# Attention in four steps per pair of heads with a fixed TensorE order, scores and masks on 64x64 quarters of the array

## The chip, the cores and the metric

One NeuronCore of a Trainium2 chip runs the whole program: TensorE (PE; its weight loads are listed as PEld), VectorE (DVE), ScalarE (ACT), GpSimd (POOL) and the queue that issues DMAs (SP). The metric is the device time of one execution in microseconds. The kernel before takes 1002.98 us (median of 3 runs, 1002.25 to 1003.76).

## The reference

Four stages follow each other: causal attention with a linear memory, gated together; a bilinear layer; its two output products; and a last layer with `h - tanh(h)`.

```python
# q, k, v: (4, 8, 576, 64); B*H = 32 heads, taken in 16 pairs
scores = scale * q @ k.T;  scores = where(causal, -1e9, scores)
a = exp(scores - max);  a /= a.sum(-1) + 1e-9;  local = a @ v
q_p = where(q > 0, q, exp(q) - 1) + 1
mem_out = (q_p @ M_prev) / (q_p . z_prev + 1e-6)
x = g * mem_out + (1 - g) * local          # rows: 2304 tokens x 512
h = ((x @ w1) * (x @ w2)) @ w3;  x = h @ w_out     # d_ff 1024
h = x @ w_in;  out = (h - tanh(h)) @ w_out2        # d_ff 2048
```

`w3 @ w_out` does not depend on the tokens; the kernel computes that product once ("the fold") while attention runs. The weights arrive as 64-bit floats and are decoded on the chip into a high and a low part (three products replace one).

## The kernel before

**Attention.** A pair P holds two heads on the two halves of the partitions. Its 576 query rows are five tiles u = 0 to 4 (four of 128 rows, one of 64), tile u sees 128 x (u+1) keys (tile 4 all 576). One unit (P, u) does: `scores` (one matmul per head, in fp32, which shows as two passes in the trace; then the causal mask is added by a matmul of a bf16 identity with a mask tile), `rmax` (DVE, L346), `exps` (ACT, L355, with its sum), `norm` (two small DVE operations L364 and L365, then POOL multiplies, L372), `trans` (transposes of the 128x128 blocks of p by PE, L404, L411 and L415; copies from PSUM into tiles g by ACT or DVE, L383 and L385) and, after tiles 1 and 4, `av` (p times v, tile o, copied out into xs). Scores have two PSUM buffers of two banks each (tile sc), the transposes two banks (t), and o shares two banks with the fold (fo).

**Shape of a matmul on the array.** The trace gives rows*columns of the array: 64*128 for the scores of tiles 0 to 3 (two heads side by side on the two row halves), 64*64 for those of tile 4, 128*128 for masks, transposes and fold, 128*64 for `av`, and 64*64 for its last block.

**The fold and other background.** A generator `early` is advanced 1.85 steps per unit: it decodes w_out and w3 (items of four steps: POOL L72 and L75, ACT L77 and L79, DVE L82, POOL L94 with DVE L97), issues the fold's matmuls (12 per item, tile fo), then decodes the first four of the 16 tiles of w1 and w2 and does the memory part of the first group of 384 tokens (tiles mw, mq, mt, mo; result added into xs on DVE, L532).

**After attention** the 2304 tokens go in six groups of 384: `stage` splits xs into xh and xl, `ab_pe` forms the products with w1 and w2 (tile ab), `ab_chain` multiplies them, `x2_pe` multiplies by the fold (tile x). Group 0 also waits for the other twelve decoded tiles of w1 and w2 (wa, wb), whose place in SBUF is attention's. Then come the last layer's two products (h and o).

**What sets the order.** The program is traced in the order of the loop over units (letters S E N T L G A with lags), and a scheduler reorders the instructions of each engine while it keeps the dependencies. So TensorE's order is the scheduler's: it fits transposes, fold pieces and the first products of group 0 between the units.

Of the kernel before, what the change touches and what calls it, by code (L numbers as in the profile page):

```python
# [33 lines left out]
def block_kernel(ctx, tc, qk, qt, vt, mp, zp_d, beta, w1, w2, w3t, wo, wi, wo2, ident_d, mask_d, out):  # L34
# [109 lines left out]

    def mm(o, lhsT, rhs, start, stop):
        return PE.matmul(o, lhsT, rhs, start=start, stop=stop).ins  # L146

    PU = 1
    PB, RB = 5, 3
    HIA, HF = 1, 1  # L150
    ZX = ("z5", "z6", "z7", "z8", "z9", "zA", "zB")
    NZ = len(ZX)
    PL = "PPPPPPPPPPG"
    HG = 4
    SB = 2
    ST = 1
    NV = "PPPPP"
    FG = 1
    G1 = 1
    DW = 1  # L160
    HIP = 1
    ORDER = "SENTLGA"
    LAG = {'S': 0, 'E': 0, 'N': 0, 'T': 1, 'L': 0, 'G': 0, 'A': 2}
    WI = ()
    PO_, PA = "xzw", "r1234"
    OP, FL = 5, "V"
    SN, XP, MR = 2, (), 0
    TH = (("V", 0), ("A", 0))
    NE, EM, BG = 4, 1, 1.85
    BG2, MB = 1.85, 40  # L170
    MS, FS, FS5 = 4, 3, 6
    CPA = (0, 1, 3, 4)

    att = ExitStack()
    PW = [256, 512, 768, 1024, 576] if PU else [1024] * 5
    apl = {}
    for x in PA:
        apl[x] = att.enter_context(tc.tile_pool(name="ap" + x, bufs={"1": 1, "2": 2, "r": RB,
                                                                     "3": 1 if PU else PB, "4": 6}[x]))
    ap1, ap2, apr, ap3, ap4 = [apl[x] for x in "12r34"]  # L180
    identb = ap1.tile([128, 128], BF16, name="identb")
    maskb = ap1.tile([128, 192], BF16, name="maskb")
# [27 lines left out]
    etags = [f"{x}{f}" for f in range(NE // 2) for x in ("wa", "wb")][len(WI):]  # L210
    otags = ztags[:4] + etags[:4]
    FO, fv = {}, {}

    def fold_o_item(j):
        def dst():
            FO[j] = slot(otags[j])
            return FO[j][:, 0], FO[j][:, 1]

        return wo[j], dst

    def fold_item(f, half):
        def dst():
            t = wslot(ap1, "zs")
            fv[f, half] = t
            return t[:, 0], t[:, 1]

        return w3t[8 * half + f], dst

    def fold_work(psum):
        seq = [("o", j) for j in range(4)]  # L230
        for f in range(8):
            if f >= OP:
                seq += [("o", 4 + f - OP)] if 4 + f - OP < 8 else []
            seq.append((f, 0))
        seq += [("o", j) for j in range(12 - OP, 8)]
        for f in range(8):
            seq += [("x", i) for i, x in enumerate(XP) if x == f]
            seq.append((f, 1))
        make = {"o": fold_o_item, "x": lambda i: w_items[i]}
        dec = Decoder([make[k[0]](k[1]) if k[0] in make else fold_item(*k) for k in seq], DW, 3)  # L240
        yield
        part = {}
        for half in range(2):
            for f in range(8):
                while dec.done <= seq.index((f, half)) or half and dec.done <= seq.index(("o", 7)):
                    dec.step()
                    yield
                acc = psum()
                t = fv.pop((f, half))
                for j in range(4):  # L250
# [5 lines left out]
                    if j % FG == FG - 1:  # L256
                        yield 1
                if half == 0:
                    part[f] = wslot(wfp, f"wf{f}", F32)
                    AC.activation(out=part[f][:, 0], in_=acc, func=AF.Copy)  # L260
                else:
                    s = ap1.tile([128, 512], F32, tag=f"s{f % SN}", name="s")
                    DV.tensor_tensor(out=s, in0=acc, in1=part[f][:, 0], op=ALU.add)
                    WF[f] = wslot(wfp, f"wf{f}")
                    AC.activation(out=WF[f][:, 0], in_=s, func=AF.Copy)
                    (DV if FL == "V" else PO).tensor_tensor(out=WF[f][:, 1], in0=s, in1=WF[f][:, 0].bitcast(F32),
                                                            op=ALU.subtract)
                    yield 2

    if True:  # L270
# [5 lines left out]
        SP.dma_start(out=mraw[:, 0:192], in_=mask_d)  # L276
# [4 lines left out]
        AC.activation(out=maskb, in_=mraw[:, 0:192], func=AF.Copy)  # L281
# [34 lines left out]
        units = [(P, u) for P in range(16) for u in range(5)]  # L316
        sc_t, p_t, st_t, g_t = {}, {}, {}, {}

        mark = {"V": {}, "A": {}}

        def scores(n):
            P, u = units[n]
            q, k = qk_t[P][:, 0], qk_t[P][:, 1]
            hr = [(h, slice(64 * h, 64 * h + 64)) for h in range(2)]
            sc = sc_t[n] = pss.tile([128, 2, 512], F32, tag="sc", name="sc")
            if u < 4:
# [5 lines left out]
            else:  # L332
# [4 lines left out]
                mm(sc[:, 1, 224:288], identb, maskb[:, 128:192], False, True)  # L337

        def seen(n):
            P, u = units[n]  # L340
            return sc_t[n][:, :, 0:128 * (u + 1) if u < 4 else 288]

        def rmax(n):
            P, u = units[n]
# [4 lines left out]
        def exps(n):  # L349
# [7 lines left out]
            sc_t.pop(n)  # L357

        def norm(n):
            P, u = units[n]  # L360
            hp = P % 4
            st, p = st_t.pop(n), p_t[n]
            w = 2 if u < 4 else 1
# [616 lines left out]
```

## Time and profile before

| | us |
|---|---|
| median of 3 runs | 1002.98 |
| profiled execution, its own time | 1002.86 |
| span from first to last instruction | 1001.1 |
| TensorE busy | 967.1 (97%) |
| VectorE, ScalarE, GpSimd busy | 661.3, 634.6, 408.9 |
| mean granted TensorE clock | 0.998 |

The profiled execution is 0.12 us from the median, and 1.8 us of it lie outside the span. Attention's scores end at 247 us, its last product with v starts at 267 us, group 0 ends at 332 us, the six groups at 598 us; the rest is the last layer. TensorE's busy time is counted from the moment an instruction holds the engine, its own weight load and the emptying of the array included, so a busy TensorE can still lose time at each change of shape.

### The profile page before, as it was taken

The numbers are of one execution on the slowest core, as the hardware profiler recorded it, in microseconds if no ns is written. First come the engines' busy times: TensorE is split into PE (matmuls) and PEld (weight loads), VectorE is DVE, ScalarE is ACT, GpSimd is POOL, SyncE is SP. The second block draws the span as 40 slices with busy tenths as digits, with TensorE's granted clock in tenths as the row PEclk, the third lists the DMA queues.
The fourth block names the chain that finished last, engine by engine and source line by source line (L and its number), as shares of the span: only waits on it lengthen the run. The fifth ranks groups of instructions, "written<-read, shape, count | busy, mean of one in ns | idle before, by whom it ended". The sixth has DMA issues, their size and how long they took to land.

```text
span 1001.1 us, 15467 instructions
## 1 busy us (share of the span) xinstructions
PE 967.1 (97%) x5512; PEld 817.0 (82%) x5512; DVE 661.3 (66%) x1185; ACT 634.6 (63%) x1428; POOL 408.9 (41%) x500
## 2 busy tenths in 40 slices
PE   6999999999998999999999999999999999999998
PEld 3565566555786888999999999999899999998996
DVE  4756666786677566442212569788887787888875
ACT  6878766798445544353213668686776777867764
POOL 5856654695367553331001884222222222222222
PEclk9999999999999999999999999999999999999999
DMA  6434533442144553132000100000000000000000
GB/s 232 159 121 138 164 115 124 127 159 64 54 158 151 158 176 106 43 109 81 2 1 1 64 22 1 1 33 1 1 32 1 1 32 1 33 1 1 32 1 32
DMA packets 25804, 68.27 MB, mean 68 GB/s; under 512 B 4864, under 2 KB 5632, under 8 KB 25728
## 3 DMA queue, kind: packets, MB, share of 16 engines
q1 hardware_dynamic: 25728, 67.29, 20.4%
q8 instruction: 43, 0.70, 0.3%
q14 instruction: 33, 0.27, 0.1%
HBM read 62.56 MB, written 4.72 MB: 67 GB/s over the span
## 4 chain that ended last, share of the span: by engine, by line
PE 85%; ACT 5%; DVE 4%; DMA 3%; POOL 1%; issue 1%; SPq 0%; DVEq 0%; ACTq 0%; POOLq 0%
PE o L146 24%; PE h L146 20%; PE ab L146 18%; PE x L146 9%; PE sc L146 5%; PE fo L146 5%; PE t L404 3%; ACT p L355 2%; DMA mw<-in_qt 2%; DVE st L346 1%; DMA r<-in_qk 1%; ACT g L383 1%; PE mo L146 1%; ACT E L79 1%; PE mo L515 1%
## 5 line engine op out<-in xcount | busy, mean ns | idle before, releaser
L860 POOL TENSOR_TENSOR gl<-s,gh 128x384 fp32r<-128x384 f32 x96 | 99.6, 1037 | 288.0 <-ACT gh L854 275.4
L372 POOL TENSOR_SCALAR p<-p,st 128x128 f32<-128x128 f32 (+2 forms) x144 | 92.0, 650 | 59.1 <-DVE st L365 28.6
L146 PE MATMUL ab<-xh,wa 128*128 128x384 f32 x384 | 108.1, 340 | 2.6 <-DVE xs L532 1.4
L146 PE MATMUL x<-abh,wf 128*128 128x384 f32 x384 | 105.8, 340 | 3.4 <-ACT abh L659 3.4
L146 PE MATMUL ab<-xh,wb 128*128 128x384 f32 x384 | 106.9, 337 | 0.1
L836 DVE SCALAR_TENSOR_TENSOR s<-s,u 128x384 f32<-128x384 f32 x96 | 84.2, 877 | 24.9 <-ACT s L826 24.0
L146 PE MATMUL sc<-r 64*64 64x288 f32 (+4 forms) x384 | 77.5, 477 | 15.9 <-ACT p L355 9.4
L355 ACT ACTIVATE p<-sc,st 128x128 f32<-128x128 f32 (+2 forms) x144 | 78.3, 551 | 20.4 <-DVE st L346 18.0
L832 ACT ACTIVATE u<-u,pc 128x384 f32<-128x384 f32 x96 | 59.4, 619 | 46.8 <-DVE s L836 46.7
L656 DVE TENSOR_TENSOR a<-ab,a 128x384 f32<-128x384 f32 x48 | 26.5, 553 | 89.2 <-PE ab L146 85.3
L346 DVE TENSOR_REDUCE st<-sc 128x2 f32<-128x256 f32 (+4 forms) x80 | 64.1, 804 | 21.7 <-PE sc L146 21.2
L146 PEld LDWEIGHTS ab<-xh,wa 128*128 128x128 f32 x384 | 70.0, 188 | 7.4 <-DVE xs L532 2.4
L146 PEld LDWEIGHTS x<-abh,wf 128*128 128x128 f32 x384 | 69.8, 187 | 5.4 <-ACT abh L659 4.3
L824 ACT ACTIVATE u<-h 128x384 f32<-128x384 f32 x96 | 46.7, 487 | 41.5 <-PE h L146 41.5
L842 DVE TENSOR_TENSOR t<-h,t 128x384 f32<-128x384 f32 x96 | 53.2, 554 | 29.8 <-ACT t L825 29.5
L75 POOL TENSOR_SCALAR E<-raw 128x512 f32<-128x512 f32 x72 | 54.8, 761 | 40.0 <-DVE z2p L82 7.6
L146 PEld LDWEIGHTS ab<-xh,wb 128*128 128x128 f32 x384 | 69.9, 188 | 1.1 <-POOL wb L94 0.7
L841 DVE SCALAR_TENSOR_TENSOR s<-s,s 128x384 f32<-128x384 f32 x96 | 63.9, 665 | 8.3
L79 ACT ACTIVATE E<-raw 128x512 uint16<-128x512 uint32 x72 | 56.8, 790 | 17.6 <-POOL E L75 17.3
L72 POOL TENSOR_SCALAR T<-raw 128x512 f32<-128x512 f32 x72 | 51.0, 708 | 39.7 <-DVE zs L97 8.7
L146 PE MATMUL x<-abl,wf 128*128 128x384 f32 x192 | 65.3, 340 | 1.2 <-DVE abl L660 1.2
L146 PE MATMUL ab<-xl,wa 128*128 128x384 f32 x192 | 64.7, 337 | 0.7 <-DVE xl L636 0.7
(214 smaller groups left out, 2569.5 us busy)
## 6 DMA issues: line engine op xcount, KB each, us to landing
raw<-in_wo SPq DMA_DIRECT2D x24, 512.0 KB, 3.7
r<-in_qk SPq DMA_DIRECT2D x15, 576.0 KB, 3.8
raw<-in_w3t SPq DMA_DIRECT2D x16, 512.0 KB, 3.5
raw<-in_w SPq DMA_DIRECT2D x16, 512.0 KB, 3.5
raw<-in_wi SPq DMA_DIRECT2D x16, 512.0 KB, 3.5
v<-in_vt SPq DMA_DIRECT2D x16, 320.0 KB, 3.5
mw<-in_qt SPq DMA_DIRECT2D x18, 256.0 KB, 2.9
out<-ob SPq DMA_DIRECT2D x18, 256.0 KB, 2.3
```

The lines of the kernel that those rows point to most:

```text
L72: PO.tensor_scalar(out=tf, in0=hw, scalar1=TOP, scalar2=-TOP, op0=ALU.min, op1=ALU.max)
L75: PO.tensor_scalar(out=e[:].bitcast(F32), in0=hw, scalar1=2.0 ** -100, scalar2=2.0 ** -53, op0=ALU.mult, op1=ALU.mult)
L79: AC.activation(out=e16, in_=lw, func=AF.Copy, scale=LOW_SCALE, bias=LOW_BIAS)
L146: return PE.matmul(o, lhsT, rhs, start=start, stop=stop).ins
L346: mark["V"][n] = DV.tensor_reduce(out=st[:, 0:2] if u < 4 else st[:, 0:1], in_=seen(n), axis=AX.X if u < 4 else AX.XY, op=ALU.max, negate= ...
L355: mark["A"][n] = AC.activation(out=p[:, x], in_=sc[:, x], func=AF.Exp, bias=st[:, x.start:x.start + 1], accum_out=st[:, 2 + x.start:3 + x. ...
L372: (DV if NV[u] == "V" else PO).tensor_scalar(out=pr, in0=pr, scalar1=sc, scalar2=1.0, op0=ALU.mult, op1=ALU.mult)
L832: AC.activation(out=u, in_=u, func=AF.Relu, bias=pc[:, 2:3])
L836: DV.scalar_tensor_tensor(out=s1, in0=s1, scalar=k2[0], in1=u, op0=ALU.add, op1=ALU.mult)
L841: DV.scalar_tensor_tensor(out=s1, in0=s2, scalar=k2[1], in1=s1, op0=ALU.add, op1=ALU.mult)
L842: DV.tensor_tensor(out=t, in0=o, in1=t, op=ALU.subtract)
L860: PO.tensor_tensor(out=l, in0=s1, in1=h[:].bitcast(F32), op=ALU.subtract)
```

## The change

The loop over 80 units becomes a loop over 64 steps, four per pair: tiles 0 and 1 together (in one score buffer, at columns 0 and 128), then 2, 3 and 4. The matmuls are no longer left to the scheduler: `pinned` marks every matmul and transpose of the attention part, and the marked ones keep the order in which they are written. A step is written as: scores, maximum, exponentials, normalisation; in the third step `av` of the previous pair's tiles 2 to 4, in the fourth `av` of this pair's tiles 0 and 1; one or two fold pieces (three matmuls each); the transposes of the step two before; then background. The fold's decoding (`fold_dec`, 2 steps of it per step, 3 in the first ten) is apart from its matmuls (`fold_pe`, which starts an item two steps after it was decoded), its decoded w3 tile has three buffers instead of one, and the last four w_out tiles have places of their own. The scores of tiles 0 to 3 are four matmuls of 64 rows and 64 columns, and the masks are matmuls on the same quarters (for the second half of the rows only its 64 columns on the diagonal). Tile g1 has two buffers instead of one.

```diff
+    def pinned(i):
+        if in_order[0]:
+            tc.keep_in_program_order(i)
+        return i.ins
+
     def mm(o, lhsT, rhs, start, stop):
-        return PE.matmul(o, lhsT, rhs, start=start, stop=stop).ins
...
+        return pinned(PE.matmul(o, lhsT, rhs, start=start, stop=stop))
+
+    def tp(o, i):
+        return pinned(PE.transpose(o, i, ident))
...
+    ZB, FLAG, WAIT = 3, 2, 2
+    PIECES = (2, 2, 1, 1)
+    PACE, LEAD = 2, 10
...
+    def fold_dec():
+        d = fdec[0] = Decoder([fold_o_item(k[1]) if k[0] == "o" else fold_item(*k) for k in fold_seq], 1, 3)
         yield
+        while d.done < d.total:
+            k = fold_seq[d.done]
+            if k[0] == "o" or len(fv) < ZB or k in fv:
+                n = d.done
+                d.step()
+                if d.done > n and k[0] != "o":
+                    folds.append((k, fstep[0]))
+            yield
+
+    def fold_pe(psum):
         part = {}
         for half in range(2):
             for f in range(8):
-                while dec.done <= seq.index((f, half)) or half and dec.done <= seq.index(("o", 7)):
-                    dec.step()
+                while not folds or folds[0][1] + FLAG > fstep[0]:
                     yield
...
+        GROUPS = ((0, 1), (2,), (3,), (4,))
...
-                K = 128 * (u + 1)
-                for h, r in hr:
-                    mm(sc[:, h, 0:K], q[r, 128 * u:128 * u + 128], k[r, 0:K], True, False)
-                for h, r in hr:
-                    mm(sc[:, h, K - 128:K], identb, maskb[:, 0:128], False, True)
...
+                K = 128 * (u + 1)
+                for h, r, y, c in qs:
+                    mm(sc[c, h, a:a + K], q[r, 128 * u + 64 * y:128 * u + 64 * y + 64], k[r, 0:K], True, False)
+                for h, r, y, c in qs:
+                    mm(sc[c, h, a + 128 * u + 64 * y:a + 128 * u + 128], identb[r, r], maskb[r, 0:128 - 64 * y], False, True)
...
-        for m in range(NU + 8):
-            for x in ORDER:
-                do(x, m - LAG[x])
...
+        for m in range(NM + 4):
+            P, s = divmod(m, 4)
+            fstep[0] = m
+            if m < NM:
+                scores(m)
+                rmax(m)
+                exps(m)
+                norm(m)
+            if s == 2 and P:
+                av(P - 1, 1)
+                if P + 1 < 16:
+                    load_v(P + 1)
+            if s == 3 and P < 16:
+                av(P, 0)
+            for _ in range(PIECES[s]):
+                next(fold, None)
+            if 0 <= m - WAIT < NM:
+                for u in GROUPS[(m - WAIT) % 4]:
+                    trans((m - WAIT) // 4, u)
...
+                    for _ in range(PACE + (m < LEAD)):
+                        next(bg, None)
...
         run(bg)
+        in_order[0] = False
```

TensorE in the last pair, where no fold is left, before (sc scores, maskb and identb the mask matmul, t transposes, o the product with v of the pair's tiles 0 and 1):

```order
L146 MATMUL sc<-r 128x256 x2
L146 LDWEIGHTS identb
L146 MATMUL sc<-maskb,identb 128x128
L146 LDWEIGHTS identb
L146 MATMUL sc<-maskb,identb 128x128
L404 MATMUL t<-ident,p 128x128 x2
L146 MATMUL o<-g_2708,v_104 64x256 x2
L146 MATMUL o<-g_2708,v_104 64x128 x2
L146 MATMUL sc<-r 128x384 x2
L146 LDWEIGHTS identb
L146 MATMUL sc<-maskb,identb 128x128
L146 LDWEIGHTS identb
```

And TensorE after, in the third step of the fourteenth pair (here o is the product with v of the thirteenth pair's tiles 2 to 4):

```order
L153 MATMUL sc<-r 64x512 x4
L153 LDWEIGHTS identb
L153 MATMUL sc<-maskb,identb 64x128
L153 LDWEIGHTS identb
L153 MATMUL sc<-maskb,identb 64x128
L153 LDWEIGHTS identb
L153 MATMUL sc<-maskb,identb 64x64
L153 LDWEIGHTS identb
L153 MATMUL sc<-maskb,identb 64x64
L153 MATMUL o<-g_2611,v_104 64x320 x6
L153 MATMUL o<-g_2611,v_104 64x192 x2
L153 MATMUL o<-g_2612,v_104 64x64 x2
```

The masks moved from two full-array matmuls, a shape of their own between the scores and the product with v, to four on the quarters that the scores use; the product with v stands directly behind the scores.

TensorE at the end of attention before (mt and mo the memory part of group 0, ab the first products of group 0):

```order
L146 MATMUL sc<-r 64x288 x4
L146 LDWEIGHTS identb
L146 MATMUL sc<-maskb,identb 128x64
L515 MATMUL mt<-ident,mw 128x128 x4
L404 MATMUL t<-ident,p 128x128 x2
L146 MATMUL mo<-mq_1497,mc 64x384 x4
L404 MATMUL t<-ident,p 128x128 x8
L146 MATMUL o<-g_2763,v_104 64x320 x6
L146 MATMUL o<-g_2763,v_104 64x192 x2
L146 MATMUL o<-g_2764,v_104 64x64 x2
L146 MATMUL mo<-mq_1498,mc 64x384 x2
L146 MATMUL ab<-xh,wa_2282 128x384
```

The same place after, from the last pair's product of tiles 0 and 1 on:

```order
L153 MATMUL o<-g_3086,v_105 64x256 x2
L153 MATMUL o<-g_3086,v_105 64x128 x2
L156 MATMUL t<-ident,p 128x128 x18
L156 MATMUL t<-ident,p 64x128
L153 MATMUL o<-g_3119,v_105 64x320 x6
L153 MATMUL o<-g_3119,v_105 64x192 x2
L153 MATMUL o<-g_3120,v_105 64x64 x2
L156 MATMUL mt<-ident,mw 128x128 x4
L153 MATMUL mo<-mq_2375,mc 64x384 x4
L153 MATMUL mo<-mq_2376,mc 64x384 x2
L153 MATMUL ab<-xh,wa_2623 128x384
L153 MATMUL ab<-xh,wb_2626 128x384
```

Before, the last pair's transposes and products with v stand among the first ab (the last product with v follows 48 of them); after, all of attention and the third mt come first.

## Rows read from the trace of the kernel before

**Rows 1.** The page: busy time of each engine, and the chain that ended last.

```profile
PE 967.1 (97%) x5512; PEld 817.0 (82%) x5512; DVE 661.3 (66%) x1185; ACT 634.6 (63%) x1428; POOL 408.9 (41%) x500
PE 85%; ACT 5%; DVE 4%; DMA 3%; POOL 1%; issue 1%; SPq 0%; DVEq 0%; ACTq 0%; POOLq 0%
```

**Rows 2.** Busy time per stretch: length, then PE, PEld, DVE, ACT, POOL; clock, DMA.

```profile
50.00:200.00 150.00, 145.48 (x928) 87.93 (x928) 97.51 (x209) 109.19 (x295) 90.05 (x136) 1.00 0.40 131
200.00:247.00 47.00, 44.31 (x339) 25.33 (x335) 35.08 (x88) 41.27 (x118) 34.81 (x51) 1.00 0.36 114
247.00:269.00 22.00, 20.42 (x146) 14.75 (x142) 13.38 (x32) 10.79 (x25) 8.61 (x9) 1.00 0.13 37
269.00:332.00 63.00, 56.83 (x333) 48.52 (x333) 47.48 (x80) 31.04 (x59) 41.47 (x47) 1.00 0.45 144
```

**Rows 3.** Timeline of PE, 137 to 151 us: start, length, line, shape, count.

```profile
137.52 0.70 PE L146 MATMUL sc<-r 64*128 64x256 f32 x4
138.16 0.28 PE L146 MATMUL sc<-maskb,identb 128*128 128x128 bf16 x2
138.28 1.04 PE L404 MATMUL t<-ident,p 128*128 128x128 f32 x8
139.25 0.92 PE L146 MATMUL sc<-r 64*128 64x384 f32 x4
...
143.71 1.13 PE L146 MATMUL sc<-r 64*128 64x512 f32 x4
144.77 0.29 PE L146 MATMUL sc<-maskb,identb 128*128 128x128 bf16 x2
...
145.21 2.42 PE L146 MATMUL o<-g,v 128*64 128x320 f32 x20
147.56 0.66 PE L404 MATMUL t<-ident,p 128*128 128x128 f32 x4
...
149.83 0.70 PE L146 MATMUL sc<-r 64*64 64x288 f32 x4
150.46 0.50 PE L146 MATMUL fo<-wa,zs 128*128 128x512 f32 x1
```

**Rows 4.** Timeline of PE, 362 to 364 us: four quarters at once.

```profile
362.46 1.52 PE L146 MATMUL mo<-mq,mc 64*64 64x384 f32 x16
363.98 0.44 PE L146 MATMUL ab<-xh,wa 128*128 128x384 f32 x1
```

**Rows 5.** Who PE waited for, 50 to 250 us: total us, times, longest.

```profile
PE sc L146 <- ACT p L355: 5.8, 12, 1.0
```

**Rows 6.** Groups by shape, 50 to 250 us: count, busy us, mean ns of one.

```profile
L383 ACT ACTIVATE g<-t 128x512 f32<-128x512 f32 x47 | 27.6, 597 | 4.6 <-PE t L404 4.3
L346 DVE TENSOR_REDUCE st<-sc 128x1 f32<-128x576 f32 x13 | 9.7, 745 | 0.8 <-PE sc L146 0.7
L355 ACT ACTIVATE p<-sc,st 128x576 f32<-128x576 f32 x13 | 9.7, 742 | 0.8 <-DVE st L346 0.8
L372 POOL TENSOR_SCALAR p<-p,st 128x576 f32<-128x576 f32 x12 | 10.0, 835 | 8.8 <-DVE st L365 8.3
```

**Rows 7.** Timeline of PE at the end of attention.

```profile
247.23 0.20 PE L146 MATMUL sc<-maskb,identb 128*128 128x64 bf16 x1
...
249.26 0.88 PE L146 MATMUL mo<-mq,mc 64*64 64x384 f32 x8 [1.06 <-ACT mq L383]
...
254.67 0.44 PE L146 MATMUL ab<-xh,wa 128*128 128x384 f32 x1
...
266.78 2.42 PE L146 MATMUL o<-g,v 128*64 128x320 f32 x20
269.13 0.66 PE L515 MATMUL mo<-ident,mw 128*128 128x128 f32 x4
```

**Rows 8.** Timeline of POOL: first and last late tile of w1 and w2.

```profile
269.38 0.62 POOL L94 TENSOR_SCALAR wa<-T 128x512 fp32r<-128x512 f32 x1 [4.60 <-PE o L146]
...
319.24 0.62 POOL L94 TENSOR_SCALAR wb<-T 128x512 fp32r<-128x512 f32 x1 [0.63 <-DVE T L82]
```

More of the change, by code (lines that the diff above doesn't have):

```diff
@@ L209, in block_kernel @@
     ztags = [f"z{i}" for i in range(5)]
-    etags = [f"{x}{f}" for f in range(NE // 2) for x in ("wa", "wb")][len(WI):]
-    otags = ztags[:4] + etags[:4]
+    otags = ztags[:4]
     FO, fv = {}, {}
@@ L222, in dst @@
         def dst():
-            t = wslot(ap1, "zs")
+            t = wslot(apz, "zs")
             fv[f, half] = t
@@ new lines, in seen, with rmax @@
+        def seen(m, u, a):
+            return sc_t[m][:, :, a:a + 128 * (u + 1) if u < 4 else 288]
+        def rmax(m):
+            P, us = step(m)
+            st = st_t[m] = ap4.tile([128, 16], F32, tag="st", name="st")
+            for x, (u, a) in enumerate(us):
+                w = 2 if u < 4 else 1
+                mark["V"][m] = DV.tensor_reduce(out=st[:, 2 * x:2 * x + w], in_=seen(m, u, a),
+                                                axis=AX.X if u < 4 else AX.XY, op=ALU.max, negate=True).ins
@@ new lines, in exps @@
+        def exps(m):
+            P, us = step(m)
+            st = st_t[m]
+            for x, (u, a) in enumerate(us):
+                sc = seen(m, u, a)
+                p = p_t[P, u] = ap3.tile([128, PW[u]], F32, tag=f"p{u}", name="p")
+                p = p[:].rearrange("p (a n) -> p a n", a=2)
+                for h in [slice(0, 1), slice(1, 2)] if u < 4 else [slice(0, 2)]:
+                    y = 2 * x + h.start
+                    mark["A"][m] = AC.activation(out=p[:, h], in_=sc[:, h], func=AF.Exp, bias=st[:, y:y + 1],
+                                                 accum_out=st[:, 4 + y:5 + y]).ins
+            sc_t.pop(m)
@@ new lines, in norm @@
+        def norm(m):
+            P, us = step(m)
+            st = st_t.pop(m)
+            w = sum(2 if u < 4 else 1 for u, a in us)
+            DV.tensor_scalar(out=st[:, 8:8 + w], in0=st[:, 4:4 + w], scalar1=1e-9, scalar2=None, op0=ALU.add)
+            DV.reciprocal(out=st[:, 12:12 + w], in_=st[:, 8:8 + w])
+            for x, (u, a) in enumerate(us):
+                K = 128 * (u + 1) if u < 4 else 576
+                for h in range(2 if u < 4 else 1):
+                    pr, sc = p_t[P, u][:, K * h:K * h + K], st[:, 12 + 2 * x + h:13 + 2 * x + h]
+                    PO.tensor_scalar(out=pr, in0=pr, scalar1=sc, scalar2=1.0, op0=ALU.mult, op1=ALU.mult)
@@ L545, in early @@
         def early():
[L546 removed]
             ps["t"] = lambda: psT.tile([128, 512], F32, tag="t", name="mt")
             ps["o"] = lambda: psA.tile([128, 512], F32, tag="o", name="mo")
[L549 to L561 removed]
+            yield from fold_dec()
+            mem_setup()
+            a, b, end = early_w(), chain(*[mem_group(g) for g in range(EM)]), object()
             while a or b:
@@ L569, in early @@
                     yield
-        NU = len(units)
-        bg, bgc = early(), [0]
-        for _ in range(ST):
-            next(bg)
+        fold = fold_pe(lambda: psA.tile([128, 512], F32, tag="o", name="fo"))
+        bg = early()
+        next(bg)
         load_qk(1)
```

222 lines of the change are left out of this document (69 added, 153 removed).

## The prediction, on record before the changed kernel ran

> **What bounds the kernel now.** I read the page's engine line and its chain first [rows 1]: TensorE is busy 967 of 1001 us, and 85% of the chain that ends last is its own work. The stretches [rows 2] say the same of attention and of what follows: from 50 to 332 us TensorE lacks 4.52 + 2.69 + 1.58 + 6.17 = 15.0 us of being always busy, at a granted clock of 1.00 throughout. So there is little idle time to win. What can be won is inside the busy time, at the changes between shapes of the array. The timeline [rows 3] shows them. From one block's start to the next one's, scores of 64*128 take .64 us for 256 columns (137.52 to 138.16), 1.06 us for 512 (143.71 to 144.77): .42 us for 256 columns more, .21 per 128, and a line through both leaves .22 us that belongs to no column. The 64*64 scores of tile 4 take .63 us for 288 columns, of which .21 x 288/128 = .47 is stream; .16 is left. Eight transposes take .97 us (138.28 to 139.25); the four at 147.56 are listed with .66, eight with 1.04, so one more costs .095 and little over .1 to .2 is left for the change. A change of shape costs about .15 us, with bounds .10 and .22 from these blocks.
>
> **Shape changes: -11.0 us.** Counted along TensorE's order up to the last product with v, without the ab that lie in it, there are 245 changes of shape before and 172 after: 15.3 and 10.75 per pair. Two things remove them. The masks now have the scores' shape, so scores, mask and mask again is one block (before, every unit went 64*128, 128*128, and on). And four steps per pair instead of five, with the fold's pieces and the transposes beside each other, leave 2, 2, 4 and 3 changes in the four steps. 73 x .15 = 11.0 us; the bounds .10 and .22 give 7.3 and 16.1.
>
> **The scores themselves: 0.** A score block of four matmuls of 64 columns each streams twice the columns of the two before. It costs nothing if the four quarters run side by side. That they do is seen later in the kernel [rows 4]: 16 passes of 384 columns in 64*64 take 1.52 us, four rounds of .38, where 16 in a row would take 5.0 (half of .21 for one pass of 128 columns, so .315 for 384). Tile 4's scores run so already in attention [rows 3]. Both ends: 0 if all overlap, and if none of it did, 1,280 columns of tiles 0 to 3 per pair x .21/128 x 16 pairs = +33.6 us. I take 0, by the nearest rows.
>
> **The masks: -1.0 us.** Before, two masks take .12 us (138.16 to 138.28) in each of the 64 units of tiles 0 to 3, with the next shape's start in it, and about .04 in 16 of tile 4: 8.3 us. After, 64 groups have four matmuls of 128 or 64 columns on the quarters, 16 have two. No row shows such short ones on quarters. If a group costs one stream of 128 bf16 columns (about .06, half the row's .12), it is 64 x .06 + 16 x .03 = 4.3 us; if its four run one after the other, 4 x .06, it is 17.3. I take .10 for a group, about 7.2 us, since the quarters of [rows 4] overlap. The bounds are -4 and +9.
>
> Here a rule of the Trainium skill speaks against the change ("TensorEngine Tiling (Array Packing)", section Instruction Overhead): each matmul has about 60 cycles of overhead, so one with few columns costs no less, and a small dimension isn't worth tiling. The kernel after issues 17 matmuls more per pair, 272 in all; at 60 cycles of 2.4 GHz that is an estimate of 6.8 us if no two of them overlap, and the sum below would be -3 instead of -10. The shortest quarter matmuls of this trace have 192 columns, so it can't show whether the rule holds for 64.
>
> **Waits inside attention: +2.1 us.** Before, 4.52 + 2.69 = 7.2 us are idle from 50 to 247 us [rows 2], 5.8 of them before a score buffer whose exponentials ACT has not finished [rows 5]. After, the order is fixed, and a wait is no longer filled by the scheduler with other matmuls; queued behind a waiting instruction is all of TensorE's work. The place that I find late is `av`. In the third step it stands behind the scores of tile 3, and the transposes whose copies it needs were issued just ahead of these: cover is 1.06 us plus the mask. In the fourth step it stands behind tile 4's scores, .63 us plus the mask [rows 3]. The copy takes .60 us on ACT [rows 6], and may find one other ACT instruction ahead (mean 109.19/295 = .37 us in [rows 2]). I take .15 us for each of the 32 products, 4.8 us; nothing if the copy starts at once, .5 if it stands behind a decoding pair. For the score buffer I take 3 us instead of 5.8: the merged step of tiles 0 and 1 gives the softmax a longer TensorE step to hide in, but its reduction and exponentials (.75 us each for 576 columns on DVE and ACT, .84 on POOL [rows 6]) still follow each other. The last three pairs have no fold on TensorE to fill; ACT is already busy 41.27 of 47 us at this place [rows 2], and I add 1.5 us. 4.8 + 3 + 1.5 = 9.3, against 7.2.
>
> **The end of attention: +3.6 us.** Before, the scheduler placed the first ab at 254.67 and the last product with v at 266.78 [rows 7]; 48 products of group 0 ran while the last softmax, the memory part and the splitting of xs were awaited, and only 1.58 us were idle from 247 to 269. After, the last 19 transposes, the last product with v and the third mt and mo come before any ab. The last scores end, one softmax has to pass (reduction .75, two small operations, exponentials .74, multiplication .84 in a row, while 6 to 14 transposes and a product with v are run): 1.2 us of wait. Then mt is copied, mo multiplied, added into xs, split into xh and xl, and only then ab starts. Between mo and the first ab there were 5.4 us before (249.26 to 254.67); the copies and the splitting that need no result of the last product with v can run under it. I take 4.0 us. 1.2 + 4.0 - 1.58 = +3.6; ends 0 and +6.
>
> **Group 0: -3.7 us.** The late tiles of w1 and w2 are written from 269.38, 4.6 us after POOL was ready, when the last product with v has freed their place, to 319.24 [rows 8]: 50 us for twelve. TensorE's 6.17 us of idle time from 269 to 332 [rows 2] are waits for them. After, the last product with v comes before all 48 ab that it followed, an estimated 8.5 of the 12.1 us between 254.67 and 266.78 [rows 7], the rest being transposes and mo, so the decoding starts that much ahead of its users. It lags by what TensorE idled for it, 6.17, so most goes; I leave 2.5, since ab itself starts late and one of the decoding's engines must do the splitting too. Ends 0 and -6.2.
>
> **The sum.** -11.0 - 1.0 + 2.1 + 3.6 - 3.7 = -10.0. The profiled execution has 1002.86 us, .12 below the median, so the forecast is 1002.98 - 10.0 = 993.0 us. Nothing outside attention and group 0 changes; the last layer keeps its time, and so does the start, where the first 25 us wait for DMAs in both. The terms' own bounds, taken as independent, add in squares to about 8 us: 985 to 1001.
>
> **The rivals.** *TensorE waits in its own order* (slower). The scheduler of before filled each wait with whatever was ready; a fixed order can't. Place: the 32 products with v, each behind ACT's copies of g, with a decoding pair ahead in ACT's queue. Price: .6 for the copy and .37 for what is ahead, less a cover already counted, so about .5 more at each, 16 us, and the time is 1009. It decides from .31 us more per product, where it has eaten the 10. For it: ACT is busy 73% of 50 to 200 us and 88% of the stretch to 247 [rows 2], and no gap can be filled. Against: DVE shares the copies and is 65% busy in the first of these stretches.
>
> *Decoding paces group 0 and moves whole* (a larger gain). If the twelve tiles, not TensorE, set the end of group 0, then group 0 ends 50 us after the last product with v whatever ab does. Before, that product is at 266.78; after, with attention 10 us shorter in TensorE's work and 8.5 us of ab out of its way, it is near 248. The end of group 0 moves by 19 to 20 us: 983. For it: the last write at 319.24 follows its DVE step by .63 in a chain. Against: TensorE is busy 56.83 of 63 us there, so it can give back only 6.17 of it.
>
> *Another engine paces attention.* The shorter TensorE work only shows the next engine: ACT at 88% in the last pairs, its copies of g 597 ns each. Then most of the 12 us of busy time comes back as idle time before t and sc, and the result is between -4 and 0, about 1001. For it: the 5.8 us before sc already wait on ACT. Against: over 50 to 200 us ACT and POOL have 41 and 60 us to spare.
>
> *The quarters don't overlap.* Then +33.6 comes on top of -10, and some time 1025 results. [Rows 4] speak against it, though for masks and scores of the same bank no row does.
>
> **How the numbers follow.** The forecast case has .49, the fixed order's waits .22, the decoding .15, the pacing engine .11, quarters that don't overlap .03. About .2% (2 us) is what a measurement of this kernel can tell from no change. Faster by more: the forecast's case with .47 of its .49, the decoding's .15, and .06 of the pacing engine's, .68 together and .02 from a mild form of the waits, so .70. Slower by more: .17 of the waits, .03 of the quarters, .01 of the rest, so .21. The same: .09. The range that leaves two in ten out goes from 980, below the decoding's 983, to 1006, which takes in the pacing engine and the milder half of the fixed order's waits. The forecast's own range is 985 to 1001.
>
> **What would show it.** TensorE's timeline in a pair should show 64*64 scores and masks as one block, about 1.0 to 1.1 us for tiles 0 and 1 together and 1.1 to 1.2 for tile 3, and the product with v right behind. If a mask group takes .24 us rather than .10, the masks' term is wrong. The waits before o on ACT's or DVE's g should be near 5 us in all from 50 to 250 us; 15 or more would be the first rival. The last scores should end near 237 us, the last product with v near 245, the first ab 4 us later, and the idle time between 269 and 332 should be gone but for a few tenths. The forecast is wrong as a whole if TensorE's busy time up to the last product with v doesn't fall by 10 us or so, or if idle time grows by as much.

## The result and the profile after

The changed kernel takes 1017.12 us (median of 4 runs, 1016.34 to 1018.32), 1.0142 times the kernel before (95% interval 1.0125 to 1.0160): 14 us slower, where 10 us faster was forecast and 1006 was the upper end of the range. The page's engine line and chain of the profiled execution (span 1014.6 us), to set beside [rows 1]:

```profile
PE 957.6 (94%) x5912; PEld 819.6 (81%) x5912; DVE 660.4 (65%) x1153; ACT 635.1 (63%) x1428; POOL 411.5 (41%) x500
PE 70%; ACT 9%; DMA 6%; DVE 6%; POOL 3%; issue 2%; SPq 0%; DVEq 0%; POOLq 0%; ACTq 0%
```

TensorE's busy time fell by 9.5 us, its idle time rose by 23.0, from 34.0 to 57.0. The gain came; waits took it, and 13.5 us more. Of the 23.0 us, 5.5 lie before 50 us, 12.7 from there to 247, 2.6 to 269, -0.9 to 332, and 3.1 behind. The windows, columns as in [rows 2], show it:

```profile
0.00:50.00 50.00, 33.61 (x288) 19.30 (x289) 28.43 (x59) 36.23 (x97) 34.01 (x56) 0.97 0.57 188
50.00:200.00 150.00, 138.87 (x1213) 88.53 (x1212) 92.04 (x190) 108.66 (x297) 92.08 (x136) 1.00 0.41 129
200.00:247.00 47.00, 38.19 (x331) 22.15 (x329) 33.22 (x69) 35.45 (x97) 31.65 (x45) 0.96 0.39 118
247.00:269.00 22.00, 17.84 (x152) 10.71 (x152) 10.11 (x25) 13.42 (x36) 8.67 (x14) 0.92 0.09 26
269.00:332.00 63.00, 57.70 (x345) 52.03 (x346) 51.93 (x88) 32.42 (x65) 43.23 (x48) 1.00 0.48 152
```

From 0 to 50 us TensorE idles 16.4 us, against 10.9 in the kernel before, whose row is this:

```profile
0.00:50.00 50.00, 39.06 (x241) 22.28 (x242) 30.42 (x68) 36.85 (x100) 33.35 (x57) 0.97 0.58 195
```

From 50 to 247 us it idles 11.1 + 8.8 = 19.9 us, before 7.2. DVE and ACT are less busy than before in the same stretches, and POOL has 58 us to spare from 50 to 200 us, so no engine has become the bound by its load. From 200 to 269 us the granted clock is below 1.00 too. What TensorE waited for, 0 to 270 us (total, times, longest), against [rows 5]:

```profile
PE o L153 <- ACT g L392: 15.0, 17, 1.8
PE sc L153 <- ACT r L195: 5.7, 2, 3.7
PE t L156 <- ACT g L392: 4.8, 7, 1.3
PE sc L153 <- ACT p L367: 4.8, 4, 2.8
PE mt L156 <- ACT g L392: 4.7, 2, 2.9
PE o L153 <- ACT p L367: 2.0, 1, 2.0
```

17.0 us stand before the products with v. (The 5.7 us for the scaled q at the start, line 195 here, are 6.5 in the kernel before.) One such place, the fourth step of a pair. TensorE:

```profile
124.78 1.09 PE L153 MATMUL sc<-r 64*64 64x512 f32 x8
125.69 0.22 PE L153 MATMUL sc<-maskb,identb 64*64 64x128 bf16 x4
125.84 2.42 PE L153 MATMUL o<-g,v 128*64 128x320 f32 x20
128.20 0.88 PE L156 MATMUL t<-ident,p 128*128 128x128 f32 x6
129.00 1.19 PE L153 MATMUL sc<-r 64*64 64x288 f32 x8
130.02 0.20 PE L153 MATMUL sc<-maskb,identb 64*64 64x64 bf16 x2
132.03 0.87 PE L153 MATMUL o<-g,v 128*64 128x256 f32 x8 [1.81 <-ACT g L392]
```

ACT in the same time:

```profile
128.22 0.69 ACT L367 ACTIVATE p<-sc,st 128x512 f32<-128x512 f32 x1 [2.02 <-DVE st L355]
...
129.56 0.62 ACT L77 ACTIVATE T<-T 128x512 f32<-128x512 f32 x1
130.08 0.77 ACT L79 ACTIVATE E<-raw 128x512 uint16<-128x512 uint32 x1
130.71 0.51 ACT L392 ACTIVATE xs<-o,omgt 128x320 f32<-128x320 f32 x1
131.11 0.87 ACT L392 ACTIVATE g<-t 128x256 f32<-128x256 f32 x2
```

And DVE:

```profile
125.62 0.69 DVE L97 TENSOR_TENSOR zs<-T,zs 128x512 fp32r<-128x512 f32 x1 [0.15 <-POOL zs L94]
126.23 0.63 DVE L375 TENSOR_SCALAR st<-st 128x2 f32<-128x2 f32 x1
126.90 0.17 DVE L376 RECIPROCAL st<-st 128x2 f32<-128x2 f32 x1
126.98 1.20 DVE L355 TENSOR_REDUCE st<-sc 128x2 f32<-128x1024 f32 x1
```

The reader is to see a ring. Tile 3's scores are complete at about 125.84. DVE comes to their maximum 1.1 us later, behind decoding and an earlier step's small operation; ACT idles 2.02 us for it, runs the exponentials, then decodes, then evacuates, and reaches the copies of the six transposes (done at 129.0) at 131.11. TensorE has only tile 4's scores between these transposes and the product, waits 1.81 us, and its next scores, which the ring starts from, are late by as much.

The end of attention, against [rows 7]:

```profile
265.78 2.42 PE L153 MATMUL o<-g,v 128*64 128x320 f32 x20 [0.58 <-ACT g L392]
268.13 0.66 PE L156 MATMUL mt<-ident,mw 128*128 128x128 f32 x4
269.26 0.88 PE L153 MATMUL mo<-mq,mc 64*64 64x384 f32 x8 [0.47 <-ACT mq L392]
271.33 0.86 PE L153 MATMUL mo<-mq,mc 64*64 64x384 f32 x4 [1.19 <-DVE xs L539]
272.12 0.44 PE L153 MATMUL ab<-xh,wa 128*128 128x384 f32 x1
```

The last product with v starts 1.0 us earlier than before, but with no ab done. The last late tile, against [rows 8]:

```profile
321.26 0.62 POOL L94 TENSOR_SCALAR wb<-T 128x512 fp32r<-128x512 f32 x1
```

### The profile page after: what moved, and what is told of

Read it like the earlier page. It is cut to its first block, busy times and chain, and to the rows that moved or that the text cites. A ratio compares the mean times of both kernels' runs of the same rounds, so it can differ in the third digit from the quotient of the medians.

```text
span 1014.6 us, 16218 instructions
## 1 busy us (share of the span) xinstructions
PE 957.6 (94%) x5912; PEld 819.6 (81%) x5912; DVE 660.4 (65%) x1153; ACT 635.1 (63%) x1428; POOL 411.5 (41%) x500
## 4 chain that ended last, share of the span: by engine, by line
PE 70%; ACT 9%; DMA 6%; DVE 6%; POOL 3%; issue 2%; SPq 0%; DVEq 0%; POOLq 0%; ACTq 0%
PE o L153 22%; PE h L153 20%; PE ab L153 16%; PE x L153 7%; DMA r<-in_qk 5%; ACT p L367 4%; DMA mw<-in_qt 2%; PE sc L153 2%; ACT E L79 2%; DVE st L355 2%; PE t L156 1%; ACT g L392 1%; ACT T L77 1%; PE fo L153 1%; POOL E L75 1%
## 5 line engine op out<-in xcount | busy, mean ns | idle before, releaser
L153 PE MATMUL sc<-r 64*64 64x128 f32 (+4 forms) x640 | 69.5, 470 | 10.5 <-ACT r L195 5.7
L75 POOL TENSOR_SCALAR E<-raw 128x512 f32<-128x512 f32 x72 | 58.1, 807 | 44.4 <-DVE z2p L82 7.5
L153 PE MATMUL o<-g,v 128*64 128x320 f32 (+4 forms) x448 | 53.6, 371 | 17.0 <-ACT g L392 15.0
L153 PEld LDWEIGHTS o<-g,v 128*64 128x64 f32 (+1 forms) x448 | 28.4, 137 | 48.8 <-ACT g L392 22.2
```

Source lines behind the costliest of these rows:

```text
L75: PO.tensor_scalar(out=e[:].bitcast(F32), in0=hw, scalar1=2.0 ** -100, scalar2=2.0 ** -53, op0=ALU.mult, op1=ALU.mult)
L153: return pinned(PE.matmul(o, lhsT, rhs, start=start, stop=stop))
```

## The experiments

"Waits" are TensorE's idle time from 50 to 247 us, each from its own window. The kernel before has 7.2, the changed one 19.9. The window is the same stretch of time in each run, not the same work (the last scores end at 247.4 us before, at 258.9 in the changed kernel and at 240.2 in e7), and it is read in one profiled execution, whose time was 3 to 5 us below the run's median in e2 and e9 and 5 us above it in e5 and e13. The ratios are to the kernel before as it ran beside each run (medians 1002.50 to 1003.10 us).

| run | edit | us | ratio to before, 95% | waits |
|---|---|---|---|---|
| e1 | both products one step later | 1002.01 | 0.9985 to 1.0004 | 9.1 |
| e2 | order not fixed | 1009.82 | 1.0044 to 1.0081 | 9.6 |
| e3 | no quarters | 1020.39 | 1.0161 to 1.0191 | 13.9 |
| e4 | before, with quarters | 1027.28 | 1.0209 to 1.0251 | 16.8 |
| e5 | product of tiles 0, 1 later | 1020.38 | 1.0137 to 1.0206 | 19.5 |
| e6 | e1, no quarters | 1012.38 | 1.0064 to 1.0104 | 5.6 |
| e7 | e1, mt later | 993.04 | 0.9871 to 0.9917 | 7.4 |
| e8 | e1, more background | 1005.73 | 1.0003 to 1.0050 | 13.9 |
| e9 | copies before decoding | 1018.97 | 1.0121 to 1.0181 | 17.4 |
| e10 | scaling of q held | 1020.24 | 1.0145 to 1.0188 | 16.6 |
| e11 | e9 and e10 | 1015.45 | 1.0101 to 1.0146 | 18.4 |
| e12 | e5, scaling held | 1007.24 | 1.0027 to 1.0056 | 11.6 |
| e13 | exponentials behind copies | 1024.96 | 1.0190 to 1.0259 | 16.7 |
| e14 | e13, scaling held | 1020.77 | 1.0160 to 1.0193 | 17.7 |
| e15 | e7, scaling held | 996.68 | 0.9923 to 0.9953 | 7.4 |
| e16 | e15, last pair free | 995.63 | 0.9905 to 0.9945 | 6.6 |
| e17 | e7, order not fixed | 1013.26 | 1.0082 to 1.0116 | |
| e18 | e7, both ends free | 995.26 | 0.9913 to 0.9947 | 6.8 |

**The products one step later (e1), or the order freed (e2).**

```diff
-            if s == 2 and P:
+            if s == 3 and P:
                 av(P - 1, 1)
...
-            if s == 3 and P < 16:
-                av(P, 0)
+            if s == 0 and P:
+                av(P - 1, 0)
# e2 instead:
-    in_order = [True]
+    in_order = [False]
```

> The changed kernel, but each product with v is written one step later: tiles 0 and 1 behind the scores of the next pair's first step, tiles 2 to 4 behind the scores of tile 4. Theory A (the products with v wait for ACT's copies of g because only one score block lies between the transposes and them; 17 us of such waits up to 270 us): the waits before o fall from 17 to under 4 us, the time falls by 11 to 16 us, to 1001 to 1006. Theory B (ACT, DVE and POOL together pace attention, whatever TensorE's order): the waits move to t and sc, the time falls by less than 4 us, to 1013 to 1017.

> The changed kernel with the scheduler free to reorder TensorE (nothing marked to keep its order); all else as changed. Theory A (a wait in a fixed order stops everything behind it): the scheduler fills the waits before o with transposes, fold pieces and first products of group 0, waits of TensorE from 50 to 250 us fall from 20 to about 8 us, some shape changes come back (about .15 us each), time 1003 to 1010. Theory B (the other engines pace attention): waits stay near 20 us, time 1014 to 1019.

e1 is 15 us faster than the changed kernel with the same fixed order: theory A's forecast. From 50 to 250 us no wait before o is left, and 150 us run almost without a gap:

```profile
50.00:200.00 150.00, 149.36 (x1308) 95.74 (x1304) 98.82 (x208) 119.54 (x328) 96.71 (x146) 1.00 0.44 139
200.00:247.00 47.00, 38.55 (x334) 22.24 (x335) 29.04 (x67) 33.17 (x93) 28.91 (x41) 0.89 0.31 93
```

ACT does more here in the same time (119.5 against 108.7 us), so theory B falls. The second row holds what is left to win inside attention. e2 gets back about half; its changes of shape up to the last product with v, counted in the trace, are 218 (186 in the changed kernel, 263 before).

**What the quarters are worth (e3, e6, e4).**

```diff
-                for h, r, y, c in qs:
-                    mm(sc[c, h, a:a + K], q[r, 128 * u + 64 * y:128 * u + 64 * y + 64], k[r, 0:K], True, False)
-                for h, r, y, c in qs:
-                    mm(sc[c, h, a + 128 * u + 64 * y:a + 128 * u + 128], identb[r, r], maskb[r, 0:128 - 64 * y], False, True)
+                for h, r in hr:
+                    mm(sc[:, h, a:a + K], q[r, 128 * u:128 * u + 128], k[r, 0:K], True, False)
+                for h, r in hr:
+                    mm(sc[:, h, a + 128 * u:a + K], identb, maskb[:, 0:128], False, True)
```

> The changed kernel with the scores of tiles 0 to 3 as two 64*128 matmuls and the masks as 128*128 (tile 4: 128*128 with 64 columns) as in the kernel before; order and steps as changed. If quarters save their shape changes (about 7 per pair at .15 us, less what the waits before o give back as they get more cover): slower than the changed kernel by 6 to 14 us, 1023 to 1031. If the short quarter matmuls cost as much as they save (rival): within 3 us of 1017.

> Both products with v one step later (1002.0 us), and the scores of tiles 0 to 3 as 64*128, masks as 128*128, as in the kernel before. With the waits for g gone, this shows what the quarters are worth by themselves. 67 changes of shape more at .15 us and masks at .12 instead of .16: 8 to 11 us slower than with quarters, 1010 to 1013. If the quarters are worth only the 3 us by which the unmoved kernel got slower: 1004 to 1006.

> The kernel before with only the scores and masks on 64*64 quarters; five steps, the scheduler's order, background as before. If quarters save one shape change per unit (80 x .1 to .15 us) and TensorE is what bounds attention: 8 to 12 us faster than before, 991 to 995. If the other engines pace attention (theory B) or the scheduler spends the time on waits: within 3 us of 1003.

With the waits before o out of the way the quarters are worth 1012.38 - 1002.01 = 10.4 us (e6), as expected. In the changed kernel only 3.3 show (e3). Its waits are 13.9 instead of 19.9, which fits longer score blocks that give the copies more cover; that this is the reason was not tried by itself. e6's block of tiles 0 and 1, then that of tile 3:

```profile
116.50 0.49 PE L153 MATMUL sc<-r 64*128 64x128 f32 x4
...
118.00 0.87 PE L153 MATMUL o<-g,v 128*64 128x256 f32 x8
...
123.62 1.13 PE L153 MATMUL sc<-r 64*128 64x512 f32 x4
124.69 0.28 PE L153 MATMUL sc<-maskb,identb 128*128 128x128 bf16 x2
124.81 1.02 PE L156 MATMUL t<-ident,p 128*128 128x128 f32 x6
```

and e1's:

```profile
112.80 0.45 PE L153 MATMUL sc<-r 64*64 64x128 f32 x8
...
113.72 0.87 PE L153 MATMUL o<-g,v 128*64 128x256 f32 x8
...
119.27 1.09 PE L153 MATMUL sc<-r 64*64 64x512 f32 x8
120.18 0.22 PE L153 MATMUL sc<-maskb,identb 64*64 64x128 bf16 x4
120.36 1.12 PE L156 MATMUL t<-ident,p 128*128 128x128 f32 x6
```

For tile 3 the scores reach the mask in .91 us with quarters, 1.07 without; the masks then take .18 instead of .12, so the block gains .10 (1.09 against 1.19). Most of the gain is in the step of tiles 0 and 1, which takes .92 us instead of 1.50: in e6 three changes of shape stand inside it. The two blocks make .68 us per pair, 10.9 in 16 pairs. The weight loads (PEld) show one thing that such a change costs. The identity for the masks is loaded at the moment that the masks start in the kernel before (144.77 in [rows 3]); in the changed kernel it is loaded .43 us ahead of them (they start at 125.69), while the scores still run:

```profile
144.77 0.11 PEld L146 LDWEIGHTS <-identb 128*128 128x128 bf16 x2 [0.76 <-issue]
...
125.26 0.13 PEld L153 LDWEIGHTS <-identb 64*64 64x64 bf16 x4 [0.28 <-issue]
```

e4 missed its forecast by over 30 us: in the kernel before, where the scheduler sets the order, quarters made it 24 us slower. The trace counts 281 changes of shape (263 before), 16.8 us of waits and a clock of 0.97 from 50 to 247 us. Over the whole span TensorE idles 11 us more and is busy 14 us more than before; the clock (0.988 against 0.998) can account for at most some 10 of these 14. The scheduler chose another order; which of its choices cost the time was not tried. So the quarters' 10.4 us are shown for the fixed order with the products moved, and not for any order.

**Only one product later (e5, e12).**

```diff
-            if s == 3 and P < 16:
-                av(P, 0)
+            if s == 0 and P:
+                av(P - 1, 0)
# e12 besides:
                 if s == 1 and P < 15:
-                    scale_q(P + 1)
+                    with tc.issue_after(mark["A"][m]):
+                        scale_q(P + 1)
```

> The changed kernel with only the product with v of tiles 0 and 1 moved one step later (behind the next pair's first scores); tiles 2 to 4 stay where the change put them. In the changed kernel 14 of 17 us of waits before o (by shape: 64*64 scores, then a product of 256 columns) stand before this one. If cover by one score block is what is short (theory A): 11 to 14 us faster than the changed kernel, 1003 to 1006, close to the run with both products moved. If it is the load of ACT (theory B), about half of that: 1009 to 1012.

> The kernel with only the product of tiles 0 and 1 one step later (1020.4 us, where ACT waited 23.5 us from 50 to 250 us for the q of a later pair), with the scaling kept behind the second step's exponentials. Theory E: ACT's DMA waits go and with them most of the 18 us that TensorE waited for g before t and o, 12 to 18 us faster, 1002 to 1008. Theory D or F: within 5 us of 1020.

e5 gained nothing. Its waits moved to the transposes (9.6 us before t for ACT's copies), because the scheduler now put the scaling of a later pair's q where its DMA had not landed, and ACT's whole queue stood behind it:

```profile
111.53 0.38 ACT L392 ACTIVATE g<-t 128x256 f32<-128x256 f32 x1
115.32 0.68 ACT L195 ACTIVATE r<-r 128x576 f32<-128x576 f32 x1 [3.41 <-DMA r<-in_qk]
115.91 0.46 ACT L392 ACTIVATE xs<-o,omgt 128x256 f32<-128x256 f32 x1
```

With the scaling held (e12) it is 13 us faster, as theory E said, and 5 us from e1. e10 below has the scaling held without the move; e12 is 13 us faster than that too. So cover for this product is worth some 10 us or more, once a second delay is out of the way.

**Other orders on ACT in the changed kernel (e9, e10, e11, e13, e14).** TensorE's order is untouched here. e10 has e12's second edit alone; e9's and e13's:

```diff
# e9 (lastc: the last copy out of PSUM on ACT and on DVE)
                         e.enter_context(tc.issue_after(mark[x][m]))
+                        if x in lastc:
+                            e.enter_context(tc.issue_after(lastc[x]))
# e13 (the same lastc)
+                if s != 2:
+                    exps(m)
+                    norm(m)
...
                     trans((m - WAIT) // 4, u)
+            if m < NM and s == 2:
+                with tc.issue_after(lastc["A"]) if "A" in lastc else ExitStack():
+                    exps(m)
+                norm(m)
```

> The changed kernel with TensorE's order untouched; only the decoding that a step issues on ACT and DVE is queued behind that step's copies out of PSUM (it stood ahead of them, T and E, 1.4 us on ACT, in each fourth step). Theory D (the waits before o are the copies' place in ACT's queue, behind the decoding pair): waits before o fall from 17 to under 7 us, 7 to 12 us faster than the changed kernel, 1005 to 1010. Theory E (ACT's queue is held by the scaling of the q of a later pair, which waits for its DMA, with everything behind it): under 4 us faster, 1013 to 1018; the scaling stands ahead of the copy of tiles 0 to 2 here as well.

> The changed kernel with TensorE's order untouched; only the scaling of the next q on ACT is kept behind the second step's exponentials, where it is written (the scheduler had put it ahead of the next pair's first exponentials, and ACT waited there 10.2 us from 50 to 250 us for its DMA). Theory D: ACT's waits for the DMA go, TensorE's waits before o stay near 15 us, 0 to 4 us faster, 1013 to 1018. Theory E: 6 to 12 us faster, 1005 to 1011.

> Both of these in the changed kernel. Theories D and E each have one part: together they take the waits inside attention to under 6 us from 50 to 247 us (20 in the changed kernel), 12 to 16 us faster, 1001 to 1005, what moving the products with v gave. If the fixed order itself is the cause (a third theory, F): still 1010 or more.

> The changed kernel with TensorE's order untouched; only in each third step ACT's exponentials of tile 3 are queued behind the copies of the transposes of tiles 0 and 1 instead of ahead of them (decoding stays behind the exponentials). Theory G (the copies stand in ACT's queue behind exponentials that wait 2 to 3 us for a late reduction on DVE; moving the decoding did not help because the exponentials still stood ahead): waits before o of 256 columns fall from 14 to under 4 us, 8 to 13 us faster than the changed kernel, 1004 to 1009. Theory F (the fixed order costs, whichever engine is late): waits reappear before sc and t, 1013 or more.

> The same, with the scaling of the next q kept behind the second step's exponentials as well. Theory G: 9 to 15 us faster than the changed kernel, 1002 to 1008; a few us better than without the scaling held. Theory F: 1013 or more.

None cures it: the times are 1015.45 to 1024.96 us, none as fast as theory D, E or G said, and waits stay between 16.6 and 18.4. e10 removed the 10.2 us that ACT waited for the DMA of a later pair's q, and gained nothing. Theories D, E (for the changed kernel) and G fall as causes by themselves, and theory F, the fixed order as such, stood until e17. e13 tells most. Its waits, 50 to 250 us:

```profile
PE t L156 <- ACT g L393: 12.7, 12, 2.2
PE mt L156 <- ACT g L393: 1.4, 1, 1.4
PE o L153 <- ACT g L393: 1.4, 3, 0.7
```

The waits before o for these copies went from 10.2 to 1.4 us, as G said, and came back before t: the exponentials are later now, and the next step's copies stand behind them. In these five runs, whatever stands first in ACT's queue, something else in the ring is late.

**The clock, the pace and the ends (e7, e8, e15 to e18).**

```diff
# e7, on e1, in mem_tok ahead of the transposes mt
             yield
+            yield
             t = ps["t"]()
# e8, on e1
-                    for _ in range(PACE + (m < LEAD)):
+                    for _ in range(PACE + (m < LEAD or m % 2)):
# e15: e7 with the scaling held. e16: e15 with this; e18: e7 with 8 <= m < NM - 4
+            in_order[0] = m < NM - 4
# e17: e7 with in_order = [False]
```

> Both products with v one step later, and one more yield between the memory part's multiplication on POOL and its transposes mt on TensorE. In the run without it TensorE waits 2.9 us for mw before one mt, and its granted clock is then 0.89 over 200 to 247 us. If that wait causes the low clock (theory C): wait gone, clock near 1.0 there, 5 to 8 us faster than 1002, 994 to 997. If the low clock comes from elsewhere: 2 to 3 us, 999 to 1000.

> Both products with v one step later, and the background at 10 steps of its generator per pair instead of 8 (2, 3, 2, 3). The fold and the memory part end earlier, so that mt, mo and the first decoded tiles of w1 and w2 are done within attention: the 4 us from the last product with v to the first ab fall below 1.5, and the 6 us from 200 to 247 us that TensorE waits on POOL and ACT shrink. Theory A: 4 to 9 us faster than 1002, 993 to 998. Theory B (the other engines pace attention; more background per pair costs more there): same or slower, 1001 to 1008.

> The fastest kernel so far (both products with v one step later, mt one yield later, 993.0 us) with the scaling of q kept behind the second step's exponentials. ACT waits there some 5 us for the q of a later pair, TensorE for none of it inside attention. If TensorE has enough cover: within 2 us of 993. If ACT's wait for DMA also costs early on: 988 to 991.

> That kernel with TensorE's order left to the scheduler from the last pair on. In the changed kernel all of attention, mt and mo stand before the first product ab, and 3.9 us pass between the last product with v and the first ab (48 ab stood there before). If the fixed order costs at the end (the prediction's term of 3.6 us): 2 to 5 us faster than with the order fixed. If what the first ab need is not there sooner anyway: within 2 us.

> The fastest kernel so far (both products with v one step later, mt one yield later, 993.0 us) with TensorE's order left to the scheduler throughout. In the changed kernel itself this gave 7 us (1017 to 1010). Theory F (a fixed order costs by itself, since a wait can't be filled): faster or equal here too, 985 to 993. Theory H (the order was not at fault, only the place of the products with v in it; with the cover there, the scheduler's own order only adds changes of shape and waits): slower, 997 to 1006, with more than 200 changes of shape up to the last product with v (188 with the order fixed).

> The same fastest kernel with the order fixed only from the third to the fifteenth pair; the first two pairs and the last are left to the scheduler. Idle time of TensorE in 0 to 50 us (16 us here, 11 in the kernel before) and after the last scores is what it can win: if the fixed order costs there, 988 to 991; if those waits are for DMAs and for the softmax itself, within 2 us of 993.

In e1 one wait of 2.87 us is followed by a stretch at the lower clock; eight transposes take 1.97 us there and 1.07 before it:

```profile
217.49 1.07 PE L156 MATMUL t<-ident,p 128*128 128x128 f32 x8 [0.89 <-ACT g L392]
...
232.37 1.12 PE L156 MATMUL mt<-ident,mw 128*128 128x128 f32 x4 [2.87 <-POOL mw L518]
...
236.59 1.97 PE L156 MATMUL t<-ident,p 128*128 128x128 f32 x8
```

A second such stretch follows at 241.8 us, behind a wait of 1.67 us. e7 has neither; the same window then reads

```profile
200.00:247.00 47.00, 40.16 (x380) 23.45 (x378) 34.42 (x78) 36.86 (x103) 33.30 (x46) 1.00 0.31 102
```

and the kernel is 9.0 us faster than e1 (theory C, a little more than it said), at 993.04 us faster than both kernels compared here. e8, with more background per pair, was slower than e1 (1001.94 to 1011.15 us in ten executions): the gap before the first ab fell from 3.9 to 1.0 us, as forecast, but there were more waits for ACT and POOL, theory B's side for once. Holding the scaling (e15) cost 3.6 us here, outside both of its forecasts. Freeing the last pair won 1.0 us (e16 against e15), within the spread of the runs; freeing both ends gained nothing (e18, 2.2 us slower than e7). e17 settles the fixed order: freed in e7, the cured kernel, it makes that 20 us slower. That is theory H's side, but 7 us beyond its 1006, and the changes of shape that H forecast are not known, since e17 left no trace of an ordinary execution.

## Why the prediction was wrong

- **Shape changes and masks, -12.0: right in the sum.** Busy time fell 9.5 us although the clock was lower (0.991 against 0.998 over the span); that cost at most some 7 us of it, so 9.5 to 17. e6 shows 10.4 for the quarters alone. The trace has 77 changes fewer (73 were counted). The masks by themselves were under-priced: a group of four takes .15 to .18 us where another shape follows (125.69 to 125.84; 120.18 to 120.36 in e1), not .10, some 2 to 4 us in the 48 groups of which this holds, within the term's bounds. By the rule of the Trainium skill weighed there ("TensorEngine Tiling (Array Packing)", Instruction Overhead) an estimated 6.8 us would have been lost; no run isolates that price, and the 10.4 us of e6 have it in them. That the shortest quarter matmuls before have 192 columns is a misreading: the last block of each product with v has 64 there.
- **Waits inside attention, +2.1: the step that failed.** They are +12.7 from 50 to 247 us: 19.9 where the term had 9.3. The place was named (the product behind tile 4's scores, ACT's copies with something ahead of them), the price was not: .15 us for each of 32 products, 4.8 in all, where 17.0 us were measured up to 270 us, mostly at the fourth step, up to 2.0 each. Of the idle time from 50 to 250 us 10.2 stand before o, and another 9.1 before t and mt, for which the term had nothing; before sc it had 3 and .5 are left. The cover was not the error: the .63 us taken for tile 4's scores are four of their eight passes, all eight take 1.02 (129.00 to 130.02), and the copies came 1.81 us too late even so. The working added one queue's head (.37 us) to one copy. It did not follow the ring around: late maximum on DVE, exponentials behind it, two copies and an evacuation behind these, and the lateness handed on to the next scores.
- **The start, 0: wrong.** Idle time in 0 to 50 us went from 10.9 to 16.4, where no change was forecast. Five of them stand before o again (2.0, .5, 1.7, .9 at 19, 30, 37 and 47 us). But e1, which has none of these, idles 16.5 there (8.0 before t), e2 without the fixed order 16.1, and e18, with the first two pairs free, 15.2. So neither the place of the products nor the fixed order explains it; the cause stays open.
- **The clock: not priced at all.** From 200 us to the last scores the lower level comes behind the two waits before mt (1.76 us up to 218.93, 2.92 up to 247.13), and in group 0 it goes with two waits of 1.44 and 1.12 us (333 to 340 us). It does not follow every wait of that length: behind the 1.81 us at 132.03 the clock stayed at 1.00. e1 against e7 shows the size: from 50 us to the last scores TensorE is busy 3.6 us less in e7 and idles 2.6 us less (187.3 and 9.1 against 183.7 and 6.5); the rest of the 9.0 comes later.
- **The end of attention, +3.6: about right, by two errors that cancel.** From the last scores (258.92) to the first ab (272.12) TensorE idles 4.8 us, +3.2 on the 1.58 before. But 3.1 of them come before the last product with v ends, where 1.2 was forecast, and in the 3.9 us behind it, taken as all idle, TensorE works 2.25.
- **Group 0, -3.7: wrong.** The last product came at 265.78, where near 245 was forecast, so decoding had no head start; its last tile is at 321.26 (319.24 before), and 269 to 332 us idles 5.3 instead of 6.2.

The first rival described what happened: it put 16 us of waits before o on top of the 4.8, some 21, and 17.0 were measured. It missed what else the ring delayed (t and mt), the start and the clock, so 1009 was still 8 short. Its reason, that a fixed order can't fill waits, is half true: freeing the order gave 7 us in the changed kernel but cost 20 in the cured one. The cause shown is the fixed order with these two products too close behind what they need: moving them, with the load of a later v that goes along, gives back 15.1 us (e1). Which single delay in the ring weighs most stays open, and so does the share of mt in the changed kernel, where its place was not moved alone: its two waits are 4.7 us, and what the clock cost behind them comes on top. That e7 ends at the forecast 993.0 is luck: it is another kernel, with 4.9 us more idle at the start than before.

## What to carry to other kernels

Before fixing an engine's order, follow each dependence once around all engines and give every instruction that waits for another engine a whole step of distance, not one instruction's length. If moving the late thing in one queue only moves the wait to another tile, the ring is too tight: change the distance, not the order. A wait on TensorE can cost more than itself, since the clock can fall behind it (2.87 us in e1), though here it did not behind each wait.

## What was unexpected of the hardware

After a wait of 2.87 us in e1 the granted clock stayed at its lower level (1.2 GHz) for some 6 us of work: eight transposes 1.97 us instead of 1.07. A wait of 1.81 us in the changed kernel (at 132.03) left it at 1.00, one of 1.76 us (at 218.93) was followed by the lower level. And the four quarters of a score block run side by side at no visible cost: a block of eight passes of 64x512 reaches its mask in .91 us, the four passes of 64*128 that do the same work take 1.07.
